# Reordering the opening, the early pairs' work and the d-weighted sums of a fused attention and two-MoE kernel

## The chip, the cores and the metric

The kernel runs on one core of a Trainium2 chip. The metric is device time in microseconds of one execution. Three executions of the kernel before took 804.86, 803.89 and 801.84 us (median 803.89). Half a percent of that is 4 us.

## The reference

Three blocks follow each other, all in float32.

```
k_p, v_p = mean of k, v over groups of 8 positions          # 8 batches, 8 heads, 576 -> 72 keys
attn     = softmax(q @ k_p.T / 8) @ v_p                     # 4608 tokens x 512 after merging heads
g        = relu(attn @ w_in) ** 2                           # 512 -> 2048
x        = g @ w_out                                        # 2048 -> 512
logits   = x @ phi                                          # 32 slots
d        = softmax of logits over the 4608 tokens
slots    = d.T @ x  ->  per expert relu(. @ w1) @ w2        # 8 experts, 4 slots each
out      = softmax(logits over the slots) @ slots
```

x itself is never needed by a token: logits are g @ (w_out @ phi) and d.T @ x is (d.T @ g) @ w_out. w_in and w_out arrive as float64 and are converted in the kernel.

## The kernel before, in words

The 4608 tokens are 36 tiles of 128 (t = 0 to 35). Attention for a tile runs in steps: att_qT (TensorE transposes of q, ScalarE copy), att_sc (scores on TensorE, maxima on VectorE, exps on ScalarE), att_norm (VectorE), att_aT and att_shift (turning the weights; on VectorE and ScalarE for t >= 12), att_av (TensorE; ScalarE makes the rounded half xh and VectorE the rest xl). The first MoE layer, h = x @ w_in, is split in four column quarters j. One tile and one quarter is a unit of 12 products (line 415, `l<-w,xh` and `l<-w,xl`): 144 units, 1728 products. Its PSUM bank has the tag l1, of which there are two. ScalarE's relu (L427) and a square, on VectorE for most units (L434), empty the bank, and SyncE stores g to DRAM (L438).

From tile 10 on, tiles go in pairs. For a pair and quarter, reload_turned brings g back in another layout, g_T turns it in blocks on VectorE (L475), and logits multiplies it by w_out @ phi on TensorE (L500). When the four quarters of a pair are in, log_T (L529) turns the logits, VectorE takes a running maximum (L532, L534), ScalarE the exps (L541), VectorE turns these into d (L544, L564), and dg (L574) adds d.T @ g on TensorE, which VectorE adds to acc (L584). log_T and dg share the one PSUM buffer `misc`. The pairs of tiles 0 to 9, here the early pairs, do this later, in between, from a copy of g read back from DRAM (`g_back`).

The order of the work is set in two stages. The loop over units runs half a unit at a time, and a table `ev` says at which of these slots (two to a unit, SLOTS = 8 to a tile) each other step is issued; post, post_end and attention fill it. The framework's scheduler then orders every engine's instructions by its own estimate, with the issue order as priority, and puts the semaphore waits in. `early` raises a priority; `behind`, `pinned` and `paced` hold a step back until a named instruction has been placed, and create no wait on the chip by themselves. Each engine runs its list in order.

The opening, before the steady loop, pools k and v of batch 0, runs attention for tiles 0 to 3 and converts the first two quarters of w_in. One conversion is one ScalarE step (L311), VectorE steps L313, L316, L320 and L325, one add (L324) that the letter in AE puts on VectorE (V) or GpSimd (P), a ScalarE cast (L363) and a GpSimd subtract (L364).

## Time and profile before

| | us |
|---|---|
| median of three executions | 803.89 |
| the profiled execution | 807.54 |
| its span, first to last instruction | 805.8 |
| TensorE busy | 754.0 (94%) |
| VectorE busy | 519.4 (64%) |
| ScalarE busy | 408.1 (51%) |
| GpSimd busy | 157.7 (20%) |

The profiled execution lies outside the span by 1.74 us and 3.65 us above the median. In the page's 40 slices of 20 us, TensorE is 60 to 70% busy in the first three and nearly full from there to the tail, which starts near 715 us. A TensorE that is called busy may still run at the lower of its two clock levels (1.2 and 2.4 GHz); the granted clock of a stretch shows that, 1.00 being the higher.

### The profile page before, as it was taken

Reading aid. Unit: us, or ns where it says so; the run is one execution under the profiler, and the core shown is the slowest. Engines: PE = TensorE matmul, PEld = TensorE weight load, DVE = VectorE, ACT = ScalarE, POOL = GpSimd, SP = SyncE. Lnnn points to the kernel's source line nnn. Section 1 sums busy time; section 2 is a strip of 40 time slices with the busy share of each in tenths; the row PEclk is TensorE's granted clock in tenths of the full one; section 3 lists DMA queues with packets and bytes.
Section 4 is the critical chain, followed back from the end, with each engine's and each line's share of the span. In section 5 each row is a group of like instructions: output and inputs, shape, how many; then the busy total and the mean of one; then the engine's idle time right before and its main releaser. Section 6 shows DMA issues by size and latency. Waiting matters only on the chain.

```text
span 805.8 us, 14370 instructions
## 1 busy us (share of the span) xinstructions
PE 754.0 (94%) x5352; PEld 521.4 (65%) x5352; DVE 519.4 (64%) x1016; ACT 408.1 (51%) x1161; POOL 157.7 (20%) x171
## 2 busy tenths in 40 slices
PE   6779999999999999999999999989999989998993
PEld 6557778767667766666667666656676756663552
DVE  5896855586827688697858677775688464324333
ACT  2755676443647364555546562654575533331232
POOL 1251412167514310071023403200000000000000
PEclk9799999999999999999999999989999999999996
DMA  8946753847835874985696696776457424969999
GB/s 258 287 144 193 233 145 124 264 125 226 260 118 159 250 220 119 297 251 145 205 293 203 180 301 187 201 220 193 118 181 249 120 79 176 349 242 321 371 372 312
DMA packets 177782, 175.07 MB, mean 217 GB/s; under 512 B 44080, under 2 KB 135216, under 8 KB 177712
## 3 DMA queue, kind: packets, MB, share of 16 engines
q1 hardware_dynamic: 177712, 174.16, 69.3%
q8 instruction: 42, 0.69, 0.4%
q14 instruction: 28, 0.23, 0.1%
HBM read 126.94 MB, written 47.19 MB: 216 GB/s over the span
## 4 chain that ended last, share of the span: by engine, by line
PE 71%; DVE 10%; DMA 8%; ACT 4%; POOL 3%; issue 2%; SPq 1%; POOLq 0%; ACTq 0%; DVEq 0%
PE l L415 42%; PE misc L574 4%; DMA kv<-in_v_dram 4%; PE pl L500 3%; PE misc L1006 2%; PE gT L280 2%; PE att L280 2%; PE gT L203 2%; PE l L974 2%; PE att L203 2%; PE att L500 2%; DMA st<-in_moe_w_in_dram 1%; DVE vp L160 1%; POOL kv L130 1%; DVE tmp L320 1%
## 5 line engine op out<-in xcount | busy, mean ns | idle before, releaser
L415 PE MATMUL l<-w,xh 128*128 128x512 f32 x1152 | 383.7, 412 | 8.5 <-DVE tmp L434 2.5
L415 PEld LDWEIGHTS l<-w,xh 128*128 128x128 f32 x1152 | 208.3, 190 | 83.1 <-issue 22.5
L415 PE MATMUL l<-w,xl 128*128 128x512 f32 x576 | 230.4, 400 | 0.0
L427 ACT ACTIVATE r<-l 128x512 f32<-128x512 f32 x144 | 86.4, 601 | 169.0 <-PE l L415 147.5
L415 PEld LDWEIGHTS l<-w,xl 128*128 128x128 f32 x576 | 108.9, 189 | 29.1 <-issue 3.7
L253 ACT COPY aT<-turned 32x256 f32<-32x256 f32 (+1 forms) x168 | 67.8, 404 | 16.7 <-DVE turned L262 14.1
L130 POOL TENSOR_TENSOR kv<-kv 72x512 f32<-72x512 f32 x40 | 53.7, 1346 | 72.1 <-DMA kv<-in_v_dram 53.2
L434 DVE TENSOR_TENSOR g<-l,r 128x512 f32<-128x512 f32 x57 | 38.8, 685 | 28.7 <-ACT r L427 20.4
L475 DVE STREAM_TRANSPOSE turned<-turned 128x1024 f32<-128x1024 f32 x39 | 47.7, 1230 | 2.9 <-DMA turned<-g_dram 2.9
L214 ACT ACTIVATE es<-gT,mx 128x72 f32<-128x72 f32 x120 | 36.9, 328 | 16.1 <-DVE mx L210 16.0
L214 ACT ACTIVATE es<-att,mx 128x72 f32<-128x72 f32 x120 | 37.0, 329 | 12.5 <-DVE mx L210 12.4
L255 DVE COPY aT<-turned 32x256 f32<-32x256 f32 (+1 forms) x120 | 40.2, 335 | 4.2 <-PE gT L280 2.3
L324 POOL TENSOR_TENSOR tmp<-tmp 128x512 f32<-128x512 f32 x20 | 28.0, 1399 | 68.5 <-DVE tmp L320 60.2
L132 POOL TENSOR_TENSOR kp<-kv 72x128 f32<-72x128 f32 x20 | 10.4, 538 | 142.8 <-PE att L173 142.7
L434 DVE TENSOR_TENSOR tmp<-l,r 128x512 f32<-128x512 f32 x33 | 22.7, 687 | 22.6 <-ACT r L427 16.6
L364 POOL TENSOR_TENSOR w<-tmp,w 128x512 fp32r<-128x512 f32 x16 | 24.8, 1562 | 55.9 <-ACT w L363 55.9
L436 ACT ACTIVATE g<-r 128x512 f32<-128x512 f32 x54 | 34.2, 636 | 0.9
L237 DVE TENSOR_TENSOR es<-es,rs 128x576 f32<-128x576 f32 x36 | 32.5, 903 | 0.8
L210 DVE TENSOR_REDUCE mx<-gT 128x4 f32<-128x288 f32 x38 | 16.5, 443 | 22.8 <-PE gT L203 22.6
L131 POOL TENSOR_TENSOR kv<-kv 72x256 f32<-72x256 f32 x40 | 30.7, 771 | 1.0
L475 DVE STREAM_TRANSPOSE tmp<-tmp 128x1024 f32<-128x1024 f32 x25 | 30.7, 1229 | 0.0
L203 PE MATMUL gT<-kb,qT 128*128 128x144 f32 (+1 forms) x176 | 26.4, 302 | 4.2 <-ACT qT L191 2.6
(188 smaller groups left out, 1139.7 us busy)
## 6 DMA issues: line engine op xcount, KB each, us to landing
g_dram<-g SPq DMA_DIRECT2D x95, 256.0 KB
turned<-g_dram SPq DMA_DIRECT2D x39, 512.0 KB
w<-in_moe_w_dram SPq DMA_DIRECT2D x32, 512.0 KB
tmp<-g_dram SPq DMA_DIRECT2D x25, 512.0 KB
w<-in_moe_w_dram SPq DMA_DIRECT2D x6, 2048.0 KB
kv<-in_k_dram SPq DMA_DIRECT2D x32, 288.0 KB
kv<-in_v_dram SPq DMA_DIRECT2D x32, 288.0 KB
out_dram<-o SPq DMA_DIRECT2D x36, 256.0 KB
```

Source lines behind the costliest of these rows:

```text
L130: eng.tensor_tensor(out=x[:, :, 0:4], in0=x[:, :, 0:4], in1=x[:, :, 4:8], op=ALU.add)
L203: mark["sc", t] = nc.tensor.matmul(sc[off:off + n, i * 2 * SP:(i + 1) * 2 * SP], qT[:, pi, off:off + n], kb[b % 2][:, pi].rearrange("p a s ...
L214: mark["es", t] = nc.scalar.activation(out=es[:, e], in_=sv[:, h], func=AF.Exp, bias=mx[:, e:e + 1], accum_out=rsum[:, t % 8, e, 0:1],)
L237: mark["norm", t] = nc.vector.tensor_tensor(out=es, in0=es, in1=rs.unsqueeze(2).to_broadcast([P, H, SP]), op=ALU.mult)
L253: nc.scalar.copy(out=dst, in_=src)
L255: eng[e].tensor_copy(dst, src)
L415: mark["l1", t, j] = nc.tensor.matmul(hp_t[t, j], steps[i][0], steps[i][1], start=(i == 0), stop=(i == 2 * n - 1))
L427: nc.scalar.activation(out=r, in_=hp, func=AF.Relu, scale=1.0 / (R * R if sq == "V" else R))
L434: mark["sq"] = nc.vector.tensor_tensor(out=dst, in0=pre, in1=src, op=ALU.mult)
L436: nc.scalar.activation(out=dst, in_=src, func=AF.Square)
L475: nc.vector.transpose(out=gc.rearrange("p (n i) -> p n i", i=32), in_=gc.rearrange("p (n f) -> p n f", f=32))
L500: mark["logits"] = nc.tensor.matmul(pl[32 * c:32 * c + 32], a_sb[:, c, 32 * j:32 * j + 32], gT[:, c], start=(alone or j == 0), stop=(alone ...
```

## The change

Seven edits, which move work and add only six warming products of the identity:

1. AE is all V: the four adds that were on GpSimd go to VectorE.
2. pool_v of batch 0 writes into a PSUM buffer of the tag l1 (two of them) and not into the one `misc`; att_qT of tile 1 is issued behind these products; six products on the identity are issued behind the transposes of tile 0's q.
3. In a slot, logits go first. Logits of an early pair are issued behind the latest logits, and the offsets of the early pairs move: g_T from 1 to 3, logits from 4 to 6, reloads from -4 to -2, dg from 22 to 23.
4. The later pairs' offsets move one slot ahead (logits 14 to 13, g_T 12 to 11, reloads 6 to 5, log_T 27 to 26, d_T 28 to 27).
5. dg of the pairs from tile 10 to before tile 28 is issued behind a first-layer product.
6. att_shift moves one slot ahead.
7. att_av, from unit slot 94 on, is issued behind the latest logits, for even tiles one slot ahead.

```diff
@@ -55,7 +55,7 @@
     EP = 3
     GO, LO = 3, 5
     PEP = (0, 1, 2)
-    AE = "VVVVVPVPPVVVVPVV"
+    AE = "V" * 16
     CS = ((2, 5, 7, 9), (13, 14, 15, 17))
 
     const = ctx.enter_context(tc.tile_pool(name="const", bufs=1))
@@ -148,9 +148,9 @@
         x = raw_v.pop((b, i))
         if b not in vp_t:
             vp_t[b] = pool.tile([SP, H, D], F32, tag="vp", name="vp", bufs=1)
-        pv = psm()[:SP, :2 * D]
+        pv = (ps("l1") if b == 0 else psm())[:SP, :2 * D]
         for r in range(R):
-            nc.tensor.matmul(pv, ident[:SP, :SP], x[:, :, r], start=(r == 0), stop=(r == R - 1))
+            mark["pv"] = nc.tensor.matmul(pv, ident[:SP, :SP], x[:, :, r], start=(r == 0), stop=(r == R - 1))
         nc.scalar.copy(out=vp_t[b][:, 2 * i:2 * i + 2].rearrange("p h d -> p (h d)"), in_=pv)
 
     def pool_v_dve(b, i, pool):
@@ -184,7 +184,7 @@
         qt = q_t.pop(t)
         pq = ps("gT" if t in (0, 2, 4, 6, 8, 10, 12, 14, 16, 18, 20, 22, 24, 26, 28, 29, 30, 31, 33) else "att")
         for i in range(NPAIR):
-            nc.tensor.transpose(
+            mark["q0"] = nc.tensor.transpose(
                 pq[:, i * P:(i + 1) * P], qt[:, 2 * i:2 * i + 2].rearrange("p h d -> p (h d)"), ident
             )
         qT = a1.tile([P, NPAIR, P], F32, tag="qT", name="qT")
@@ -343,6 +343,7 @@
 
     wq = []
     last_relu = []
+    last_l1 = []
 
     def paced(fn, *a):
         with tc.issue_after(last_relu[-1].ins):
@@ -412,7 +413,8 @@
         ]
         n = len(steps) // 2
         for i in range(half * n, (half + 1) * n):
-            mark["l1", t, j] = nc.tensor.matmul(hp_t[t, j], steps[i][0], steps[i][1], start=(i == 0), stop=(i == 2 * n - 1))
+            mm = mark["l1", t, j] = nc.tensor.matmul(hp_t[t, j], steps[i][0], steps[i][1], start=(i == 0), stop=(i == 2 * n - 1))
+        last_l1.append(mm)
         if half == 1:
             hp = hp_t.pop((t, j))
             if j == NQ - 1 and ND <= t < NT - 4:
@@ -712,19 +714,26 @@
             fn(*a)
 
     def run_slot(s):
-        for fn, a in ev.pop(s, []):
+        for fn, a in sorted(ev.pop(s, []), key=lambda e: e[0] is not logits):
             if fn in (g_T, logits, log_T, d_T, dg) and a[0] >= NT - EP:
                 early(fn, *a)
             else:
                 fn(*a)
 
+    def behind_l1(fn, *a):
+        with tc.issue_after(last_l1[-1].ins):
+            fn(*a)
+
     def pinned(name, fn, *a):
         with tc.issue_after(mark[name].ins):
             fn(*a)
 
     def post(t, s0, o, step=4):
         for j in range(NQ):
-            at(s0 + step * j + o[1], logits, t, j)
+            if t < ND:
+                at(s0 + step * j + o[1], pinned, "logits", logits, t, j)
+            else:
+                at(s0 + step * j + o[1], logits, t, j)
         for j in range(NQ):
             at(s0 + step * j + o[0], pinned, "sq", g_T, t, j)
             at(s0 + step * j + o[2], pinned, "store", reload_turned, t, j)
@@ -732,7 +741,10 @@
     def post_end(t, s0, p):
         at(s0 + p[0], log_T, t)
         at(s0 + p[1], d_T, t)
-        at(s0 + p[2], dg, t)
+        if ND <= t < NT - 8:
+            at(s0 + p[2], behind_l1, dg, t)
+        else:
+            at(s0 + p[2], dg, t)
 
     def attention(t, a0):
         if t >= NT - 4:
@@ -748,8 +760,11 @@
         at(a0 + 2, att_exp, t)
         at(a0 + 2, att_norm, t)
         at(a0 + 4, att_aT, t)
-        at(a0 + 6, att_shift, t)
-        at(a0 + 7, att_av, t)
+        at(a0 + 5, att_shift, t)
+        if a0 + 6 + t % 2 < 8 * ND + 14:
+            at(a0 + 7, att_av, t)
+        else:
+            at(a0 + 6 + t % 2, pinned, "logits", att_av, t)
 
     a_at = {4: 24, 5: 26}
     for t in range(6, NT):
@@ -779,8 +794,8 @@
         attention(t, a_at[t])
     for t in range(ND, NT - 2, 2):
         if t < NT - 4:
-            post(t, SLOTS * t, (12, 14, 6))
-        post_end(t, SLOTS * t, (27, 28, 28))
+            post(t, SLOTS * t, (11, 13, 5))
+        post_end(t, SLOTS * t, (26, 27, 28))
     for t in (NT - 4, NT - 2):
         s0 = SLOTS * t
         for i in range(2):
@@ -799,8 +814,8 @@
     for t in range(0, ND, 2):
         s0 = 96 + 28 * (t // 2)
         at(s0 - 5, reload_g, t)
-        post(t, s0, (1, 4, -4), 4)
-        post_end(t, s0, (20, 21, 22))
+        post(t, s0, (3, 6, -2), 4)
+        post_end(t, s0, (20, 21, 23))
     for b in range(1, B):
         s0 = a_at[b * S // P]
         for i in range(NPAIR):
@@ -871,6 +886,9 @@
         early(kb_from, 0, pk0)
         go(0, 0, 2)
         early(att_qT, 0)
+        warm = ps1.tile([P, P], F32, tag="pl", name="warm")
+        for _ in range(6):
+            behind(["q0"], nc.tensor.matmul, warm, ident, ident)
         go(0, 0, 1)
         behind([("qT", 0), "kbA"], go, 0, 0, 1)
         early(att_sc, 0)
@@ -890,7 +908,7 @@
         behind([("aT", 0)], go, 0, 3, 1)
         for half in range(2):
             l1_half(0, 0, half)
-        att_qT(1)
+        behind(["pv"], att_qT, 1)
         behind([("aT", 0)], att_sc, 1)
         att_norm(1)
         behind([("l1", 0, 0)], att_aT, 1)
```

TensorE, in the opening, from the scores of tile 0 to those of tile 1. `gT_262` and `att_381` are score buffers, `misc_291` and `misc_302` pooled v. Before:

```order
L203 MATMUL gT_262<-kb0_119,qT_255 128x144 x2
L203 MATMUL gT_270<-kb0_119,qT_255 128x144 x2
L153 MATMUL misc_291<-kv0_148,ident_93 72x128 x8
L187 MATMUL att_373<-ident_93,qt_155 128x128 x4
L153 MATMUL misc_302<-kv0_148,ident_93 72x128 x8
L203 MATMUL att_381<-kb0_119,qT_378 128x144 x2
L203 MATMUL att_389<-kb0_119,qT_378 128x144 x2
```

And in the changed kernel:

```order
L627 MATMUL warm_257<-ident_93 128x128 x6
L203 MATMUL gT_269<-kb0_119,qT_255 128x144 x2
L203 MATMUL gT_277<-kb0_119,qT_255 128x144 x2
L153 MATMUL l1_298<-kv0_148,ident_93 72x128 x8
L153 MATMUL l1_309<-kv0_148,ident_93 72x128 x8
L187 MATMUL att_380<-ident_93,qt_155 128x128 x4
L203 MATMUL att_388<-kb0_119,qT_385 128x144 x2
L203 MATMUL att_396<-kb0_119,qT_385 128x144 x2
```

Both poolings of v now stand ahead of the transposes of tile 1's q, and the six products stand ahead of the first scores.

TensorE, between units 103 and 104 of the first layer (near 526 us in the trace), where log_T and dg of the pair of tile 22 meet the attention of two tiles. Before:

```order
L203 MATMUL gT<-kb_119,qT 128x144 x4
L529 MATMUL misc<-plsb,s4rep 128x256
L187 MATMUL gT<-ident,qt 128x128 x4
L203 MATMUL gT<-kb_119,qT 128x144 x4
L574 MATMUL misc<-g,d 32x512 x2
L574 MATMUL misc<-tmp,d 32x512 x2
L574 MATMUL misc<-g,d 32x512 x3
L574 MATMUL misc<-tmp,d 32x512
```

And in the changed kernel, where the sums of an early pair (`g_back`), one unit earlier before, stand between the transposes of q and the scores:

```order
L203 MATMUL gT<-kb_119,qT 128x144 x4
L531 MATMUL misc<-plsb,s4rep 128x256
L187 MATMUL gT<-ident,qt 128x128 x4
L576 MATMUL misc<-g_back,d 32x512 x8
L203 MATMUL gT<-kb_119,qT 128x144 x4
L576 MATMUL misc<-g,d 32x512 x2
L576 MATMUL misc<-tmp,d 32x512 x2
L576 MATMUL misc<-g,d 32x512 x3
L576 MATMUL misc<-tmp,d 32x512
```

VectorE at the same place, from the scaling of one tile's exps (es0) to the square that gives unit 104 its PSUM bank (l1_5186 before, l1_5199 now). Before:

```order
L237 TENSOR_TENSOR es0_121<-es0_121,rs_5296 128x576
L210 TENSOR_REDUCE mx_5335<-gT_5336 128x4
L262 STREAM_TRANSPOSE turned_2429<-es0_121 128x768
L210 TENSOR_REDUCE mx_5335<-gT_5344 128x4
L434 TENSOR_TENSOR tmp_124<-l1_5186,r_5216 128x512
L255 COPY aT_5389<-turned_2429 32x8x32 x3
L255 COPY aT_5389<-turned_2429 8x8x32 x2
L584 SCALAR_TENSOR_TENSOR acc_101<-acc_101,scl_5179,misc_5198 128x512
```

And in the changed kernel:

```order
L237 TENSOR_TENSOR es0_121<-es0_121,rs_5306 128x576
L262 STREAM_TRANSPOSE turned_2436<-es0_121 128x768
L586 SCALAR_TENSOR_TENSOR acc_101<-acc_101,scl_5107,misc_5186 128x512
L255 COPY aT_5375<-turned_2436 32x8x32 x3
L255 COPY aT_5375<-turned_2436 8x8x32
L210 TENSOR_REDUCE mx_5343<-gT_5344 128x4
L255 COPY aT_5375<-turned_2436 8x8x32
L210 TENSOR_REDUCE mx_5343<-gT_5352 128x4
L436 TENSOR_TENSOR tmp_124<-l1_5199,r_5222 128x512
```

The five copies stood behind the square and now stand ahead of it, with an addition to acc (that of the early pair).

## Rows read from the trace of the kernel before

**Rows 1.** The page: the span, and busy time of each engine.
```profile
span 805.8 us, 14370 instructions
PE 754.0 (94%) x5352; PEld 521.4 (65%) x5352; DVE 519.4 (64%) x1016; ACT 408.1 (51%) x1161; POOL 157.7 (20%) x171
```

**Rows 2.** Windows: length, busy us (instructions) by engine, granted clock, DMA.
```profile
0.00:63.00 63.00, 44.63 (x403) 36.34 (x403) 46.64 (x87) 33.59 (x96) 19.62 (x27) 0.92 0.72 220
...
230.00:715.00 485.00, 477.09 (x3022) 321.42 (x3021) 326.60 (x681) 255.35 (x747) 72.85 (x90) 0.99 0.65 200
...
20.40:56.60 36.20, 26.92 (x162) 20.49 (x162) 32.92 (x57) 23.80 (x78) 13.29 (x10) 0.86 0.68 214
```

**Rows 3.** Timeline of TensorE, opening: start, us, instruction, idle before and releaser.
```profile
21.74 1.11 PE L187 MATMUL att<-ident,qt 128*128 128x128 f32 x4 [3.99 <-DMA qt<-in_q_dram]
24.91 3.69 PE L153 MATMUL misc<-kv,ident 72*72 72x128 f32 x16 [2.05 <-ACT vp L154]
...
62.95 1.19 PE L415 MATMUL l<-w,xh 128*128 128x512 f32 x4 [0.89 <-ACT xh L287]
```

**Rows 4.** Windows of 2 us in the opening, for the granted clock.
```profile
24.00:26.00 2.00, 1.09 (x5) 1.10 (x6) 1.76 (x3) 1.35 (x5) 1.21 (x1) 0.50 0.99 288
```

**Rows 5.** Timeline of VectorE, opening.
```profile
12.43 0.69 DVE L324 TENSOR_TENSOR tmp<-tmp 128x512 f32<-128x512 f32 x1
...
15.65 1.64 DVE L324 TENSOR_TENSOR tmp<-tmp 128x512 f32<-128x512 f32 x1
...
35.88 1.74 DVE L325 SCALAR_TENSOR_TENSOR tmp<-tmp 128x512 uint32<-128x512 uint32 x1
...
55.17 1.40 DVE L237 TENSOR_TENSOR es<-es,rs 128x576 f32<-128x576 f32 x1
```

**Rows 6.** Timeline of GpSimd at the same times.
```profile
35.79 1.28 POOL L364 TENSOR_TENSOR w<-tmp,w 128x512 fp32r<-128x512 f32 x1 [1.47 <-ACT w L363]
...
54.29 1.66 POOL L324 TENSOR_TENSOR tmp<-tmp 128x512 f32<-128x512 f32 x1 [2.09 <-DVE tmp L320]
```

**Rows 7.** Timeline of TensorE near 110 us, before unit 16.
```profile
112.55 1.14 PE L280 MATMUL att<-aT,vp 72*64 72x128 f32 x16 [0.59 <-ACT aT L269]
```

**Rows 8.** Timeline around 562 us: a chain from log_T to d without a queue.
```profile
561.71 0.63 PE L415 MATMUL l<-w,xh 128*128 128x512 f32 x2
562.17 0.60 PE L529 MATMUL misc<-plsb,s4rep 128*128 128x256 f32 x2
...
565.44 0.74 DVE L564 STREAM_TRANSPOSE d<-dT 32x64 f32<-32x64 f32 x3
```

**Rows 9.** Timeline between units 103 and 104, the pair of tile 22.
```profile
519.65 1.92 PE L574 MATMUL misc<-g_back,d 128*32 128x512 f32 x16
...
527.72 0.66 PE L187 MATMUL gT<-ident,qt 128*128 128x128 f32 x4 [0.98 <-ACT es L214]
...
530.05 2.29 PE L203 MATMUL gT<-kb,qT 128*128 128x144 f32 x8 [1.68 <-ACT qT L191]
...
534.27 0.69 DVE L434 TENSOR_TENSOR tmp<-l,r 128x512 f32<-128x512 f32 x1 [0.28 <-PE misc L574]
...
534.88 1.46 DVE L255 COPY aT<-turned 32x256 f32<-32x256 f32 x5
...
535.84 0.97 PE L415 MATMUL l<-w,xh 128*128 128x512 f32 x2
...
536.37 0.75 DVE L584 SCALAR_TENSOR_TENSOR acc<-acc,scl,misc 128x512 f32<-128x512 f32 x1
```

**Rows 10.** A window of 4 us at the same place, for the granted clock.
```profile
532.00:536.00 4.00, 4.00 (x19) 0.76 (x17) 3.65 (x9) 3.14 (x13) 0.00 (x0) 0.50 0.04 9
```

**Rows 11.** Timeline around unit 128, the pair of tile 28.
```profile
642.46 0.59 PE L529 MATMUL misc<-plsb,s4rep 128*128 128x256 f32 x2
...
648.56 0.62 PE L574 MATMUL misc<-g,d 128*32 128x512 f32 x2 [1.22 <-DVE d L564]
...
651.71 0.74 PE L415 MATMUL l<-w,xh 128*128 128x512 f32 x2 [1.22 <-DVE tmp L434]
```

## The prediction

> **What bounds the kernel now.** The page comes first: TensorE is busy 754.0 of 805.8 us and no other engine comes near [rows 1]. The windows by stage come second, since that share is an average. In the steady stretch from 230 to 715 us TensorE is busy 477.09 of 485 us; in the first 63 us it is busy 44.63, and there VectorE is busy longer, 46.64 [rows 2]. So two regimes matter. In the opening VectorE's list sets the pace: from 20.4 to 56.6 us it is busy 32.92 of 36.2 us [rows 2]. In the steady part every us of TensorE's idle time, and every stretch at the lower clock level, lands in the end; all other work there is hidden. Third is TensorE's timeline, for idle times with their releasers. In the opening the reader is to see 3.99 us before the transposes of tile 1's q and 2.05 us before the second pooling of v, and then that pooling taking 3.69 us [rows 3], at a granted clock of 0.50, the lower level [rows 4]. In the steady part two places stand out: between units 103 and 104 idle times of 0.98 and 1.68 us [rows 9], and at unit 128 two of 1.22 us [rows 11]. The change touches all of these. The end of the kernel, from the last pairs on, keeps its order and counts as nothing.
>
> **Opening, edits 1 and 2.** Seen from TensorE alone much goes: the second pooling moves into the wait for q, and the scores of tile 1, which stood behind it, no longer wait. But the first dense unit group starts at 62.95 us behind xh of tile 3 [rows 3], and this comes at the end of VectorE's list. So I sum that list over 20.4 to 56.6 us, to the last of the four scalings (L237). By the changed order the same piece holds three more adds (L324, 0.69 us each [rows 5]) and two more last steps L325, which stood just behind the piece before; I price these at 0.65: 3.4 us more. Against that, VectorE is drawn out while GpSimd works: an L325 takes 1.74 us beside a GpSimd subtract of 1.28 us, and a scaling 1.40 us beside a GpSimd add of 1.66 us [rows 5, 6]. Against some 0.7 us undisturbed, as the add at 12.43 us [rows 5], that is 1.0 and 0.7 us. Three GpSimd adds leave the piece, 2.1 to 3.0 us less. Last, VectorE's idle time there was 36.2 - 32.92 = 3.3 us; in the changed list I find some 0.7 us, for the exps of tile 0 end earlier. The piece becomes 3.4 - (2.1 to 3.0) - 2.6 = -1.3 to -2.2 us by this sum. Some of it is lost behind it: ScalarE's list now has two turned tiles, two squares and two casts ahead of xh of tile 3. I take -0.8. The bounds: -4.0, if the wait of 3.99 us for q turns wholly into gain, and +3.0, since the changed list puts xl of tile 0 behind nine more VectorE operations, of 0.36 to 0.69 us and one lengthened, while ScalarE gives xh no earlier. The six warming products stand where TensorE waits for the copies of the pooled k, so at no cost; they have a quarter of the columns of a first-layer product, which takes 0.23 us (two in 0.46 [rows 8]), and without that cover I estimate 1.5 us at most.
>
> The rows show the delay beside GpSimd as 0.7 to 1.0 us an operation [rows 5, 6]. The Trainium skill ("SBUF — State Buffer", "Who interferes with whom") says that a VectorE instruction with two SBUF inputs and a GpSimd instruction that reads SBUF exclude each other for the whole instruction. By that rule the moved adds have the same exposure to the subtracts that stay, and the trace agrees: the add at 15.65 us took 1.64 us [rows 5]. By the rule alone a GpSimd operation could cost VectorE its full 1.28 to 1.66 us, three of them 3.8 to 5.0, and the piece would be shorter by 3.0 to 4.2 us; by the rows it is the -1.3 to -2.2 above.
>
> **Unit 16.** The average over v of one tile waits 0.59 us for its turned weights [rows 7]. In the changed order these weights are turned later: only nine of sixteen products of another average (0.65 us of 1.15) and four transposes (0.66) stand between. The wait grows by up to 0.9 us; I take +0.6, bounds 0 and +0.9.
>
> **The pair of tile 12 (unit 64), edits 3 to 5.** log_T of this pair slips behind an early pair's sums, since both need `misc`, and dg follows after 3.4 us of TensorE work: one average (1.14 us [rows 7]), four short transposes, log_T itself and seven products at 0.23 us. Before, there were over 7 us between. A chain from log_T to d without a queue takes from 562.17 to 566.18, 4.0 us [rows 8]; where exps stand in its way, 642.46 to 648.56, 6.1 us [rows 11]. The wait is 0.6 us at least and 2.7 at most. VectorE's list holds only the chain itself there, so I take +0.6.
>
> **The pair of tile 22 (units 103 and 104).** Before, dg followed log_T by two steps of attention alone, and unit 104 began at 535.84 us [rows 9]. The sums of the early pair (1.92 us at 519.65 [rows 9]) now fill the wait for the scaled q, which was 1.68 us. But unit 104 needs the PSUM bank that the square at 534.27 empties, and by the changed list five copies (1.46 us) and an addition to acc (0.75 us) come ahead of that square [rows 9]. Without its 0.28 us of idle time the square would end at 534.27 + 0.69 - 0.28 + 1.46 + 0.75 = 536.9 us, 1.05 us after unit 104's old start; with 1.92 us of work already in, the net is -0.9. TensorE would then stand idle for some 3 us in front of unit 104, where before it worked, at the lower level (0.50 [rows 10]). Before, that level fell on a stretch which waited anyway; now it may fall on dense products. A window of 4 us at 0.50 costs 2 us, two of them 4. Bounds -0.9 and +3.0; I take +0.7, nearer to the row of 0.50, with most of one such window.
>
> **The pair of tile 28 (unit 128).** log_T stood 12 products and little else ahead of dg, 3.7 us of TensorE work; now 22 products, two score steps and four logits, 6.3 us, more than the 6.1 us that the chain took [rows 11]. The first 1.22 us go. The second was a square queued behind d, the turn of a tile and its copies; in the changed list the square stands ahead of these. Both go: -2.4, and -1.2 if the square is late.
>
> **The rest.** Edit 4 keeps six slots between a reload and its turn, so the DMAs have the time they had. The turns of an early and a later pair now fall into one slot and stand side by side on VectorE; the square behind them has a second PSUM bank as cover. Price nothing, at most 1.5 us over the whole part.
>
> **Sum.** -0.8 + 0.6 + 0.6 + 0.7 - 2.4 = -1.3 us. The profiled execution took 807.54 us with a span of 805.8; it becomes 806.2. It stood 3.65 us above the median of three, and I set the change against that median: 803.89 - 1.3 = 802.6 us.
>
> **Rivals.** What a measurement can tell from no change is 0.5%, 4 us: below 799.9 or above 807.9 us.
>
> First, the opening really shrinks. TensorE's chain for tile 1 and half of the time at the lower level go, and xh of tile 3 comes near 59 us. For it: 6 us of waits in [rows 3] are removed by name. Against it: VectorE's busy 91% of the piece. Price -4.0 in place of -0.8, and the pair of tile 22 at -0.9: 803.9 - 6.1 = 797.8 us.
>
> Second, slower, at one place: VectorE's list in front of unit 104. If the attention of the second tile keeps the square until after 537 us and the idle TensorE falls to the lower level for two windows, the term is +3.0, and the same pattern of copies ahead of squares, which the changed list shows at two more places (pairs of tiles 12 and 14, 9 us of VectorE work between two squares, by my count of the list, for 7 before), costs 1.5 each. Then 803.9 - 1.3 + 2.3 + 3.0 = 807.9, and above it if the low stretch is longer. It decides from 6 us of idle time and slow products at the three places together, since the other terms sum to -2.0. Against it: before, runs of 8 to 10 us of VectorE work between squares showed no wait at other places.
>
> Third, the adds are not paid back. If GpSimd's subtracts, now four in a row, draw out the moved adds as the one at 15.65 us, and tile 0's xl is late, the opening is +3.0: 806.4 us, with one of the waits above at its upper end 808.
>
> **How the numbers follow.** Forecast, all near their middle: 0.44. First rival 0.32. Second 0.17, third 0.07. So faster 0.32, same 0.44, slower 0.24. The range runs from just under the first rival, 797.0, to just above the second, 808.5; beyond them I leave 0.2. The likeliest case alone has 800 to 806.
>
> **What would show it.** Right: the first dense group starts between 60 and 64 us; at unit 128 no wait above 0.4 us for d or for a square; a wait for a square of 2 to 4 us in front of unit 104. Wrong: the dense group starts before 60 us; no wait in front of unit 104 at all; or new waits of TensorE for d or a square above 1.5 us between 340 and 500 us. The prediction fails if any one place moves more than 4 us.

## The result, and the profile after

The kernel after took 796.42 us (median of four executions, 794.55 to 799.82) beside 804.38 for the kernel before: a ratio of 0.9912, 95% interval 0.989 to 0.9934. Timed again later (e9 below), it took 796.76 us, ratio 0.9882 (0.9859 to 0.9905). By the medians it is faster by 8.0 us, and by 9.4 in e9. The forecast, 802.6, was too high, and the time is 0.6 us below the foot of the range. Of all executions below one, of e6, took 1800.86 us and is left out of that kernel's ratio.

First the page's busy times of the profiled execution, which took 799.82 us:

```profile
PE 753.3 (94%) x5364; PEld 528.1 (66%) x5364; DVE 515.6 (65%) x1020; ACT 407.1 (51%) x1161; POOL 149.8 (19%) x167
```

TensorE is busy as long as before [rows 1] in a span that is 7.8 us shorter. The windows that answer to [rows 2] (length, busy us of TensorE, its loads, VectorE, ScalarE and GpSimd, then granted clock):

```profile
0.00:63.00 63.00, 51.07 (x418) 42.74 (x419) 46.44 (x94) 34.11 (x98) 16.51 (x25) 0.84 0.76 229
230.00:707.00 477.00, 470.11 (x3018) 321.28 (x3017) 325.86 (x681) 254.89 (x747) 73.60 (x90) 1.00 0.67 203
20.40:56.60 36.20, 28.45 (x169) 21.94 (x168) 36.13 (x66) 24.15 (x80) 10.09 (x8) 0.86 0.72 230
```

In the first 63 us TensorE stands idle for 11.9 us, where it was 18.4, but at a mean clock of 0.84 for 0.92: part of the filled time is work at the lower level. Its busy time there is 6.4 us longer than before [rows 2], so that behind the first 63 us it is some 7 us shorter. VectorE is now busy without a gap in the piece of the opening that the prediction summed, 36.13 of 36.2 us. TensorE's timeline of the opening, for [rows 3]:

```profile
26.28 1.25 PE L203 MATMUL att<-kb,qT 128*128 128x144 f32 x8 [1.51 <-ACT qT L191]
...
29.86 1.47 PE L268 MATMUL gT<-ident,es 128*72 128x128 f32 x8 [2.33 <-DVE es L237]
...
62.19 1.20 PE L416 MATMUL l<-w,xh 128*128 128x512 f32 x4
```

The wait of 3.99 us for the q of tile 1 is gone, and the pooling of 3.69 us no longer stands behind it; 1.51 and 2.33 us stand near by instead, the second for VectorE. The first dense group starts at 62.19 us for 62.95. The places of [rows 7] and of the pair of tile 12 (unit 64):

```profile
111.05 1.14 PE L280 MATMUL att<-aT,vp 72*64 72x128 f32 x16
...
341.66 0.62 PE L576 MATMUL misc<-g,d 128*32 128x512 f32 x2 [0.69 <-ACT r L429]
```

The wait of 0.59 us at unit 16 is gone, and one of 0.69 us stands in front of dg at unit 64. Between units 103 and 104, for [rows 9]:

```profile
524.59 0.66 PE L187 MATMUL gT<-ident,qt 128*128 128x128 f32 x4 [0.98 <-ACT es L214]
...
527.41 2.39 PE L576 MATMUL misc<-g_back,d 128*32 128x512 f32 x16 [2.16 <-DVE lt_sb L546]
...
531.95 0.69 PE L576 MATMUL misc<-g,d 128*32 128x512 f32 x2
...
534.12 0.73 PE L416 MATMUL l<-w,xh 128*128 128x512 f32 x2 [0.18 <-DVE tmp L436]
```

Here the 1.68 us for the scaled q has become 2.16 us in front of the early pair's sums (`g_back`), which cannot start until VectorE has turned the logits of the later pair out of `misc`. In front of unit 104 only 0.18 us are left (0.94 in the trace of e9), for this square:

```profile
533.38 0.69 DVE L436 TENSOR_TENSOR tmp<-l,r 128x512 f32<-128x512 f32 x1
```

Two windows of 4 us there, for [rows 10]:

```profile
527.00:531.00 4.00, 3.59 (x21) 1.77 (x22) 3.82 (x10) 0.77 (x2) 0.00 (x0) 0.72 0.26 58
531.00:535.00 4.00, 3.82 (x25) 1.87 (x24) 3.83 (x10) 3.93 (x19) 0.00 (x0) 0.86 0.91 291
```

The granted clock there is 0.72 and 0.86, where [rows 10] had 0.50. Around unit 128, for [rows 11]:

```profile
633.47 0.70 PE L531 MATMUL misc<-plsb,s4rep 128*128 128x256 f32 x2
...
641.22 0.62 PE L576 MATMUL misc<-g,d 128*32 128x512 f32 x2
```

dg follows log_T by 7.75 us of other work and waits for nothing; the next first-layer products do not wait either.

Counted by the starts of units (12 first-layer products each, in TensorE's timeline), the two profiled executions differ like this: unit 4 starts 2.1 us earlier, unit 44 0.4, unit 100 1.8, unit 135 7.5, and the rest of the kernel keeps that. So in this pair of traces nearly all is gained between units 44 and 135, and 5.8 us of it behind the start of unit 104 (1.7 us earlier).

### The profile page after: what moved, and what is told of

It reads as the page before. It is cut to its first block, busy times and chain, and to the rows that moved or that the text cites. A ratio compares the mean times of both kernels' runs of the same rounds, so it can differ in the third digit from the quotient of the medians.

```text
span 798.0 us, 14389 instructions
## 1 busy us (share of the span) xinstructions
PE 753.3 (94%) x5364; PEld 528.1 (66%) x5364; DVE 515.6 (65%) x1020; ACT 407.1 (51%) x1161; POOL 149.8 (19%) x167
## 4 chain that ended last, share of the span: by engine, by line
PE 75%; DVE 9%; DMA 6%; ACT 3%; issue 3%; POOL 2%; SPq 1%; ACTq 0%; DVEq 0%; POOLq 0%
PE l L416 44%; PE pl L502 3%; PE misc L576 3%; PE gT L280 2%; PE misc L1024 2%; DMA kv<-in_v_dram 2%; PE att L280 2%; PE l L992 2%; PE gT L203 2%; DMA kv<-in_k_dram 2%; PE att L203 2%; PE att L137 2%; PE att L502 2%; DMA qt<-in_q_dram 1%; PE misc L531 1%
## 5 line engine op out<-in xcount | busy, mean ns | idle before, releaser
L255 DVE COPY aT<-turned 32x256 f32<-32x256 f32 (+1 forms) x120 | 37.5, 312 | 4.0 <-PE gT L280 2.3
L365 POOL TENSOR_TENSOR w<-tmp,w 128x512 fp32r<-128x512 f32 x16 | 22.9, 1433 | 70.2 <-ACT w L364 70.2
L313 DVE TENSOR_SCALAR tmp<-tmp 128x512 uint32<-128x512 uint32 x32 | 22.4, 701 | 16.8 <-ACT tmp L311 16.7
L324 POOL TENSOR_TENSOR tmp<-tmp 128x512 f32<-128x512 f32 x16 | 21.1, 1321 | 62.2 <-DVE tmp L320 62.2
L237 DVE TENSOR_TENSOR es<-es,rs 128x576 f32<-128x576 f32 x36 | 30.1, 837 | 0.9
L311 ACT ACTIVATE tmp<-st 128x512 f32<-128x512 f32 x32 | 21.4, 672 | 13.6 <-DMA st<-in_moe_w_in_dram 9.5
```

Source lines behind the costliest of these rows:

```text
L255: eng[e].tensor_copy(dst, src)
```

## The experiments

Twelve kernels ran, in three groups of four, each with the kernel before beside it. All numbers of a stretch below go from the start of unit 44 to the start of unit 135 (the first-layer products 529 and 1621 in TensorE's order) of the kernel's own profiled execution, so each holds the same work. "Breaks" counts, in TensorE's list of instructions, how often the run of first-layer products is left for other products in that stretch.

### The opening against the rest: e1 and e2

e1 is the kernel before with edits 1 and 2 (its diff cut to the lines that do the work):

```diff
-    AE = "VVVVVPVPPVVVVPVV"
+    AE = "V" * 16
-        pv = psm()[:SP, :2 * D]
+        pv = (ps("l1") if b == 0 else psm())[:SP, :2 * D]
...
+        for _ in range(6):
+            behind(["q0"], nc.tensor.matmul, warm, ident, ident)
...
-        att_qT(1)
+        behind(["pv"], att_qT, 1)
```

> The kernel before with edits 1 and 2 alone (the adds on VectorE, the opening's buffers, order and six warm products); the later units as before. The first theory (the opening gives about 2 us at unit 4, and the rest of the gain of 8 us comes from the stretch behind 230 us): unit 4 starts 2 us earlier, at most 2 us of it is left at the end, so about 802.5 us beside 804.4, a ratio of 0.997 to 1.000. The rival that the opening gives nearly all: about 797 us, ratio 0.991.

Measured: 801.18 us, ratio 0.9962 (0.9939 to 0.9985). e2 is the rest, edits 3 to 7 of the diff, on the opening of before (cut in the same way):

```diff
+        for fn, a in sorted(ev.pop(s, []), key=lambda e: e[0] is not logits):
...
+                at(s0 + step * j + o[1], pinned, "logits", logits, t, j)
...
+            at(s0 + p[2], behind_l1, dg, t)
...
+        at(a0 + 5, att_shift, t)
...
+            at(a0 + 6 + t % 2, pinned, "logits", att_av, t)
...
+            post(t, SLOTS * t, (11, 13, 5))
...
+        post(t, s0, (3, 6, -2), 4)
```

> The kernel before with edits 3 to 7 alone (order of logits, av, turn and sums with d); the opening as before. The first theory: unit 44 to unit 135 take 6.5 to 7.5 us less, as in the kernel after, so about 797.5 us, ratio 0.990 to 0.993. The rival that the opening gives nearly all: about 803.5 us, ratio 0.998 to 1.000.

Measured: 797.08 us, ratio 0.9914 (0.9887 to 0.9941), as good as the whole change. TensorE's list in the stretch is the same in e2 and in the kernel after, so the first theory holds: the first rival of the prediction (the opening) does not carry the result. By itself the opening does give something, and more than the first theory allowed (a ratio of 0.9962, where it had 0.997 at the least). But e1's executions fall in two halves: six at a mean granted clock of 0.977 to 0.982 took 798.4 to 800.2 us, six at 0.970 to 0.976 took 802.1 to 805.7, and the profiled one is of the second half.

In e1 the stretch also took only 420.7 us, with the order of before, whose own profile has 423.8. So a single trace of before is some 2 us high in this stretch, and what the edits do must be read against several traces with the old order: 420.7 in e1, 421.3 and 422.8 in e3 and e4 below, mean 421.6.

### The two parts of the opening: e3 and e7

```diff
# e3: edit 1 alone
-    AE = "VVVVVPVPPVVVVPVV"
+    AE = "V" * 16
# e7: edit 2 alone, the other lines of e1
```

> The kernel before with edit 1 alone: the seven adds of the opening that GpSimd made are on VectorE. First theory: VectorE is the busier engine of the opening with them, but what the first units wait for is no longer behind GpSimd, so unit 4 starts 1 to 2 us earlier and the time falls by 0 to 2 us, ratio 0.9975 to 1.000; edit 2 then adds at most 1 us to it. Rival: the adds alone are not hidden on VectorE, the time rises by 1 to 4 us, ratio 1.001 to 1.005, and edit 2 with its warm products and order is what pays.

> The kernel before with edit 2 alone (the pooling of v in the l1 buffers, q of tile 1 behind it, six warm products). First theory (VectorE's list sets the opening): unit 4 starts within 1 us of the kernel before, since the three GpSimd adds and what they draw out stay; about 804 us, ratio 0.9985 to 1.001. Rival (TensorE's chain for tile 1 sets it): unit 4 starts 2 to 4 us earlier, 801 us, ratio 0.995 to 0.9975.

(The letters of AE move four adds, not seven.) Measured: e3 803.31 us, ratio 0.9985 (0.9964 to 1.0005); e7 805.43, ratio 1.001 (0.9989 to 1.0031). By time neither alone can be told from no change. In the traces unit 4 starts at 62.7 us in e3 and at 67.0 in e7; with the opening of before it starts between 65.7 and 68.2 us (five traces). Edit 2 alone gives nothing that can be measured, as the first theory had it. But e7 is not the old order behind the opening: the scheduler gave TensorE another list in the stretch, although the edit stands in the opening. In its trace both waits at unit 128 are gone, without an edit there, and a wait for a square of the kind that the prediction feared stands in front of unit 104:

```profile
534.37 1.22 PE L415 MATMUL l<-w,xh 128*128 128x512 f32 x2 [2.85 <-DVE tmp L434]
...
638.83 0.60 PE L529 MATMUL misc<-plsb,s4rep 128*128 128x256 f32 x2
...
647.21 0.62 PE L574 MATMUL misc<-g,d 128*32 128x512 f32 x2
```

The stretch takes 421.5 us all the same. So the two waits of unit 128 can go and the kernel be no faster.

With both edits, unit 4 starts anywhere between 61.8 and 67.2 us, and e1 shows why. The end of VectorE's list there, the start of the dense group, and three windows:

```profile
51.87 0.76 DVE L237 TENSOR_TENSOR es<-es,rs 128x576 f32<-128x576 f32 x1
```

```profile
62.27 2.08 PE L415 MATMUL l<-w,xh 128*128 128x512 f32 x4
```

```profile
0.00:20.00 20.00, 15.57 (x206) 14.63 (x206) 10.14 (x28) 5.99 (x15) 3.94 (x16) 1.00 0.91 266
56.00:64.00 8.00, 7.78 (x66) 6.52 (x63) 3.02 (x6) 3.50 (x8) 1.26 (x1) 0.53 0.49 135
64.00:68.00 4.00, 4.00 (x13) 3.12 (x13) 1.93 (x1) 0.18 (x1) 0.00 (x0) 0.67 0.09 7
```

VectorE's last scaling ends at 52.6 us, 4 us earlier than before (55.17 + 1.40, [rows 5]): the shortening that the first rival wanted. But from 56 to 68 us TensorE runs at 0.53 and 0.67, four products take 2.08 us and not 1.19 [rows 3], and unit 4 starts at 67.2 us as if nothing had been gained. In e3 the window from 56 us is at the full clock:

```profile
58.70 1.20 PE L415 MATMUL l<-w,xh 128*128 128x512 f32 x4 [1.05 <-ACT xh L287]
```

```profile
56.00:64.00 8.00, 6.95 (x85) 5.68 (x82) 6.82 (x9) 4.05 (x10) 2.83 (x2) 1.00 0.71 209
```

Here the dense group starts at 58.7 us, near the 59 of the first rival. Of the six traces with both edits three have the low stretch behind 56 us (e1, e10, e11, to within 0.1 us of each other). In the two of the kernel after it falls early, in the first 20 us,

```profile
0.00:20.00 20.00, 16.45 (x170) 15.88 (x171) 5.78 (x22) 5.02 (x8) 3.96 (x16) 0.75 0.89 257
56.00:64.00 8.00, 7.25 (x88) 5.84 (x89) 5.11 (x8) 5.54 (x12) 2.71 (x2) 1.00 0.50 131
```

and there VectorE's last scaling ends at 56 to 57 us. In one, e8, neither happens, and unit 4 starts at 61.8 us. What decides where the lower level falls was not tried.

### Edit 5 alone: e4

```diff
+        if ND <= t < NT - 8:
+            at(s0 + p[2], behind_l1, dg, t)
...
```

> The kernel before with edit 5 alone: the product for dg of tiles 10 to 27 is issued behind a first-layer product. First theory (the gain of the later stretch is spread: fewer changes between first-layer and other products, a higher clock at unit 104, one wait): this edit alone changes less than 2 us, ratio 0.9975 to 1.001. Rival (the gain is the removed waits at units 104 and 128 alone, which edit 5 takes away by itself): unit 104 starts 3 us or more earlier relative to unit 100, and the time falls by 3 to 6 us, ratio 0.9925 to 0.996.

Measured: 803.96 us, ratio 0.9994 (0.9977 to 1.0011). The two waits of 1.22 us at unit 128 are still there in its trace, the same to the hundredth. The rival falls.

### Edits 3 and 4, and edits 6 and 7: e5, e6 and e11

```diff
# e5: edits 3 and 4
-            post(t, SLOTS * t, (12, 14, 6))
-        post_end(t, SLOTS * t, (27, 28, 28))
+            post(t, SLOTS * t, (11, 13, 5))
+        post_end(t, SLOTS * t, (26, 27, 28))
-        post(t, s0, (1, 4, -4), 4)
+        post(t, s0, (3, 6, -2), 4)
# e6: edits 6 and 7; e11: these with edits 1 and 2
-        at(a0 + 6, att_shift, t)
-        at(a0 + 7, att_av, t)
+        at(a0 + 5, att_shift, t)
+        if a0 + 6 + t % 2 < 8 * ND + 14:
+            at(a0 + 7, att_av, t)
+        else:
+            at(a0 + 6 + t % 2, pinned, "logits", att_av, t)
```

> The kernel before with edits 3 and 4 alone (logits first in a slot, early pairs' logits behind the latest logits, offsets moved; later pairs one slot ahead). First theory (the waits): the two waits of 1.22 us at unit 128 go with the earlier log_T and the earlier square, and nearly all of the gain of the middle edits sits there, so units 100 to 135 take 170 to 171 us beside 173.3 to 175.3 in the kernels with the old order, and the time is 799 to 801 us, ratio 0.993 to 0.996. Rival (the grouping of the attention steps): these edits take 2.4 us off unit 128 and give it back elsewhere, 803 us, ratio 0.998 or more.

> The kernel before with edits 6 and 7 alone (att_shift one slot ahead; att_av behind the latest logits, even tiles one slot ahead). First theory (the waits): the two waits of 1.22 us at unit 128 stay; fewer changes between first-layer and other products give 0.5 to 1.5 us, about 803.5 us, ratio 0.998 to 1.000. Rival (the grouping of the attention steps is what pays): L187, L203 and L280 take 1.7 us less between units 100 and 135, first-layer products 1 us less, and with the same elsewhere the time is 799 to 801 us, ratio 0.993 to 0.996.

> The kernel before with edits 1, 2, 6 and 7: the kernel after without edits 3 to 5. First theory (the attention's edits carry the stretch from unit 44 to 135, 417.4 us alone for 417.0 with edits 3 to 5, and edits 3 to 5 add nothing to them): the same time as the kernel after within 1.5 us, ratio 0.988 to 0.9925. Rival (the effects add: 0.9952 for edits 3 and 4 and 0.9923 for 6 and 7): 3 us or more slower than the kernel after, ratio 0.992 to 0.995.

Measured: e5 801.41 us, ratio 0.9952 (0.9932 to 0.9973); e6 798.71, ratio 0.9923 (0.9896 to 0.995); e11 797.33, ratio 0.9887 (0.9861 to 0.9913), beside 0.9882 for the kernel after on the same chip. So the attention's two edits give most by themselves, both parts remove the same waits, and edits 3 to 5 add nothing measurable to edits 6 and 7. The first theory of e6 (the waits stay, ratio 0.998 or more) fell. In e6, where log_T and dg kept their slots, the waits at unit 128 are gone too:

```profile
633.42 0.70 PE L529 MATMUL misc<-plsb,s4rep 128*128 128x256 f32 x2
...
641.18 0.62 PE L574 MATMUL misc<-g,d 128*32 128x512 f32 x2
...
643.04 0.50 PE L415 MATMUL l<-w,xh 128*128 128x512 f32 x1
```

log_T stands 7.8 us ahead of dg, where [rows 11] had 6.1. And the long wait at unit 104 comes with edits 3 and 4 (edit 3 moves the early pair's sums); in e5 it is the same 2.16 us, with the sums behind it slower (3.64 us for 2.39 in all, the first half of them shown here) at a clock of 0.50:

```profile
528.47 1.93 PE L574 MATMUL misc<-g_back,d 128*32 128x512 f32 x8 [2.16 <-DVE lt_sb L544]
```

```profile
528.00:532.00 4.00, 3.53 (x16) 0.68 (x16) 3.79 (x12) 0.71 (x2) 0.00 (x0) 0.50 0.27 60
```

This is where edits 3 to 5 lose what they gain. Units 100 to 105 take 28.4 us in e6 and e11, at a granted clock of 1.00, and 32.0 and 32.7 in the kernel after and e9, where one stretch at the lower level falls there (0.6 us of the difference is a logits group that falls on this side of unit 100). The rest of the stretch takes 387.4 and 388.9 us in e6 and e11, and 384.6 and 384.2 in the kernel after and e9.

### What a break costs: e8, e9 and e10

e8 is the kernel after with the four logits products of a later quarter cut in two:

```diff
+        if split(t):
+            logits_mm(t, j, 0, 2)
+        else:
+            logits_mm(t, j, 0, 4)
+            logits_out(t, j)
+    def logits_rest(t, j):
+        with tc.issue_after(last_l1[-1].ins):
+            logits_mm(t, j, 2, 4)
+        logits_out(t, j)
+                at(s0 + step * j + o[1] + 1, logits_rest, t, j)
```

> The kernel after, with the four logits products of each quarter of the pairs from tile 10 to before tile 32 cut in two halves, the second one slot later behind a first-layer product: no product added, 44 more breaks in the run of first-layer products. First theory (each change from first-layer products to others and back costs about 0.1 us and 0.1 us of TensorE, which is how the kernel after saves time without a wait): 44 x 0.21 = 9 us more than the kernel after, 804 to 806 us, ratio to before 1.000 to 1.003; first-layer and logits products in the trace take that much longer. Rival (a change costs nothing beyond the products' own time, the shorter times are an accident of which records show): 796 to 798 us, ratio 0.990 to 0.993.

Measured: 812.38 us, ratio 1.0103 (1.007 to 1.0136), slower than either theory. It does not tell them apart: most halves landed beside other work, so that the list has only nine breaks more, and the time went elsewhere. The busy time of the logits in the stretch, in e8 and in the kernel after:

```profile
251.57:684.13 432.56, 57.02 (x536) 15.64 (x536) 1.00 0.65 195
```

```profile
257.26:673.93 416.67, 43.98 (x536) 12.34 (x536) 1.00 0.68 203
```

and one quarter whole in the kernel after, with the first-layer products around it, two halves in e8:

```profile
325.81 0.63 PE L416 MATMUL l<-w,xh 128*128 128x512 f32 x2
326.27 0.40 PE L416 MATMUL l<-w,xl 128*128 128x512 f32 x1
326.60 0.64 PE L502 MATMUL pl<-turned,a_sb 128*32 128x256 f32 x8
327.17 0.73 PE L416 MATMUL l<-w,xh 128*128 128x512 f32 x2
327.73 0.40 PE L416 MATMUL l<-w,xl 128*128 128x512 f32 x1
```

```profile
323.16 0.63 PE L514 MATMUL pl<-turned,a_sb 128*32 128x256 f32 x4
...
325.31 0.62 PE L514 MATMUL pl<-turned,a_sb 128*32 128x256 f32 x4
```

Half of the products takes as long as all: 0.63 us for four records, 0.64 for eight (a product leaves two records). The four products of a quarter, each to 32 output partitions of its own, run beside each other; cut apart, they lose that, 57.02 - 43.98 = 13.0 us of busy time in the stretch. The Trainium skill ("TensorE: Matmul & The Clock Gate", "Part 3: Packing small matmuls — row/col tiling") says that products on different 32-column tiles of the array overlap; these rows agree.

e10 goes the other way, two quarters at a time; e9 is the kernel after beside it.

```diff
-                at(s0 + step * j + o[1], logits, t, j)
+                at(s0 + step * (j | 1) + o[1], logits, t, j)
```

> The kernel after with the logits of the pairs from tile 10 to before tile 32 two quarters at a time (the first of two waits four slots for the second): the same products, and in the order of TensorE 147 breaks in the run of first-layer products in place of 163. First theory (each break costs 0.2 to 0.3 us of TensorE, as the 14 fewer between units 44 and 135 of the kernel after went with 4.2 us less of busy time): 3 to 5 us less than the kernel after, units 44 to 135 in 413.5 to 415.5 us, with first-layer products 2 us or more below 273.3. Rival (breaks cost nothing by themselves; only waits and the attention's own steps count): the same as the kernel after within 1 us, or slower where a turned tile is held longer and its reload waits.

> The kernel after once more, timed on the same chip as the three kernels beside it: ratio to before 0.989 to 0.993, units 44 to 135 in 417 to 419 us.

Measured: e10 794.44 us, ratio 0.9868 (0.9845 to 0.9892); e9 796.76, ratio 0.9882. The stretch: all of TensorE, then its first-layer products alone, in e1 (order of before), after, e9 and e10.

```profile
256.11:676.83 420.72, 415.23 (x2648) 278.84 (x2646) 297.53 (x630) 226.28 (x670) 61.70 (x78) 1.00 0.66 201
```

```profile
256.11:676.83 420.72, 285.71 (x1093) 197.39 (x1093) 1.00 0.66 201
```

```profile
257.26:673.93 416.67, 410.84 (x2648) 280.25 (x2646) 299.24 (x630) 226.17 (x670) 63.42 (x78) 1.00 0.68 203
```

```profile
257.26:673.93 416.67, 282.10 (x1093) 198.43 (x1093) 1.00 0.68 203
```

```profile
256.21:673.06 416.85, 410.42 (x2647) 279.51 (x2646) 298.76 (x630) 226.30 (x670) 63.08 (x78) 1.00 0.67 202
```

```profile
256.61:672.50 415.89, 412.32 (x2647) 281.26 (x2646) 298.91 (x630) 226.67 (x670) 63.34 (x78) 1.00 0.68 203
```

```profile
256.61:672.50 415.89, 277.90 (x1092) 199.53 (x1093) 1.00 0.68 203
```

The first-layer products, the same 1092 in each (a row can count one more at its edge), were busy 285.71, 282.10 and 277.90 us with 116, 102 and 86 breaks. All kernels but e8, by the same two rows each:

| kernel | breaks | stretch, us | TensorE idle | first-layer busy |
|---|---|---|---|---|
| before | 116 | 423.8 | 6.8 | 285.9 |
| e1, e3, e4 (old order) | 116 | 420.7, 421.3, 422.8 | 5.5, 5.8, 7.2 | 285.7, 285.7, 285.7 |
| e7 (edit 2) | 116 | 421.5 | 6.2 | 287.2 |
| e6, e11 (edits 6, 7) | 113 | 415.7, 417.2 | 3.2, 4.6 | 284.7, 284.7 |
| e5 (edits 3, 4) | 107 | 419.1 | 4.6 | 283.4 |
| e2, after, e9 | 102 | 415.6, 416.7, 416.9 | 5.3, 5.8, 6.4 | 282.1, 282.1, 282.1 |
| e12 (without edit 2) | 98 | 414.9 | 4.9 | 281.0 |
| e10 | 86 | 415.9 | 3.6 | 277.9 |

From 116 to 86 breaks the first-layer time falls from 285.7 to 277.9 us, 0.26 us a break, and no kernel leaves the line by more than 0.3 us but e7, where the lower level fell on first-layer products of unit 104. Since the end of a busy row overlaps the start of the next, I also summed from start to start without the idle times: 274.3 us at 116 (e1, e3, e4), 271.8 at 102, 269.7 at 86, which is 0.15 us a break. The rows around one quarter above show it: within the run two products take 0.46 us from start to start (325.81 to 326.27), but the one before the logits leaves 0.33 us for 0.23 and the first two behind them take 0.56 (327.17 to 327.73).

That a break costs the first-layer products 0.15 us or more is shown. That the kernel gains as much for each break that goes is not. With 16 breaks fewer than e9, all of TensorE in e10 was busy 1.9 us longer (412.32 for 410.42), its logits alone 47.85 us for 43.98, because they were taken apart in more places. Its stretch is 1.0 us shorter than that of e9 only by idle time, and the lower level did not fall there at all. The theory's 3 to 5 us did not come, and by time e10 cannot be told from the kernel after. And e6, with 113 breaks, needs no longer for the stretch than the kernel after with 102.

### Without edit 2: e12

```diff
# the kernel after, with these put back
+        pv = psm()[:SP, :2 * D]
+        att_qT(1)
# and without mark["q0"], mark["pv"] and the six warm products
```

> The kernel after without edit 2 (edits 1 and 3 to 7). First theory (edit 2 gives nothing, as alone, 1.001; the adds on VectorE give the little that the opening gives): the same time as the kernel after within 1.5 us, unit 4 at 63 to 65 us, ratio 0.988 to 0.9925. Rival (edit 2 pays once the adds are moved, 0.9962 for both beside 0.9985 for the adds alone): 2 us slower, ratio 0.992 to 0.995.

Measured: 794.96 us, ratio 0.9869 (0.9846 to 0.9893), the same as the kernel after within the intervals. Unit 4 starts at 63.6 us. Edit 2 pays nothing that can be measured; as in e7, the order of the stretch changed with it (98 breaks for 102).

## Why the prediction was right and wrong

The likeliest case had the direction right and the size wrong: it gave -1.3 us, which it counted as no change, and the kernel is faster by 8.0 us (9.4 in e9), about 1%. The first rival's 797.8 us lies near the measured 796.42 by luck: it put 4 us on the opening, and e2 is as fast without the opening's edits.

**The step that failed is "The rest. Price nothing."** The prediction went through the waits of TensorE and called all its other time fixed. Read against three traces with the old order (e1, e3, e4), the stretch went from 421.6 to 416.8 us (after and e9); the idle time in it did not change, 6.2 us before and 6.1 after. The whole 4.8 us is busy time: first-layer products 285.7 to 282.1, logits 45.0 to 44.0, averages over v (L280) 29.1 to 28.05, these being busy sums that overlap a little. The first part goes with the fewer breaks, 14 at 0.17 (start to start) to 0.26 us, 2.4 to 3.6 us. That the shorter logits and averages have the same cause was not tried by itself. Nor is this the only way to the same time: in e6 and e11 the gain is in good part idle time (3.2 and 4.6 us) and the clock at unit 104, with three breaks fewer than before. The diff said it plainly: logits first in a slot, early logits behind later ones, averages behind logits put three kinds of work side by side, and I read that only for whom it makes wait.

**The opening, -0.8.** Right in the profiled execution, but by luck: the dense group is 0.76 us earlier there, and 0.4 us later in e9 (63.34 us), the same kernel. The working was not right. The sum for VectorE's list, -1.3 to -2.2, was too small: where TensorE's first 20 us run at the full clock, the list ends 4 us earlier (e1), and the lower level takes that back later. The prediction had the lower level as a cost only at unit 104. Of the drawing out I said 0.7 to 1.0 us for each GpSimd operation. The kernel after shows it on other instructions, first VectorE's, then GpSimd's:

```profile
25.85 1.42 DVE L316 TENSOR_SCALAR tmp<-tmp 128x512 uint32<-128x512 uint32 x1
...
52.30 1.30 DVE L324 TENSOR_TENSOR tmp<-tmp 128x512 f32<-128x512 f32 x1
```

```profile
25.65 1.34 POOL L365 TENSOR_TENSOR w<-tmp,w 128x512 fp32r<-128x512 f32 x1 [6.04 <-ACT w L364]
...
51.59 1.46 POOL L365 TENSOR_TENSOR w<-tmp,w 128x512 fp32r<-128x512 f32 x1 [2.22 <-ACT w L364]
```

Of the nine subtracts between 18 and 58 us seven have such an instruction beside them, 0.4 to 1.0 us longer than its like; one of them is a moved add. Each of the seven ends a fixed time behind the subtract that was running when it began: 0.28 us for L313 and L316 (27.27 behind 26.99 in the rows above), 0.55 us for L320, L324 and L325 (53.60 behind 53.05). So it waits for the rest of the subtract, and there is no price for each GpSimd operation; its loss depends on how much of the 1.26 to 1.65 us is left when it comes. The Trainium skill ("SBUF — State Buffer", "Who interferes with whom") says that whichever of the two engines comes first holds the ports that they share for its whole instruction, while the other waits; these rows agree. The prediction took from that rule a full operation each, which is its upper bound.

**Unit 16, +0.6:** wrong, no wait is left there (111.05 us). **Unit 64, +0.6:** the size is right, 0.69 us; the profile puts it down to a relu on ScalarE and not to d, so the reason is not confirmed.

**The pair of tile 22, +0.7:** the wait of 2 to 4 us came, but at another place and for another reason. I forecast it in front of unit 104 for a square. It stands in front of the early pair's sums, 2.16 us, because log_T and the sums share the one `misc` buffer, a fact that the prediction used at unit 64 and forgot here. The square itself ended at 533.38 + 0.69 = 534.1 us and cost 0.18. Beside the old order the place is worth nothing: units 100 to 105 take 32.0 us (32.7 in e9), and 31.9 to 32.0 in e1, e3 and e4 (33.3 in the trace of before, where the low level at [rows 10] fell longer). Beside e6 and e11, with 28.4, it costs some 3 us. The second rival's slower case did not come as a whole.

**The pair of tile 28, -2.4:** right in size and place; both waits went. But e6 shows that the averages' new place does it as well as the earlier log_T, which the prediction gave as the cause, and in e7 they went without either.

**New waits, within "at most 1.5 us":** the removed 2.4 us at unit 128 were matched by others, 0.69 us at 341.66, 2.16 for 1.68 at unit 104, smaller ones, and one for pooled v from GpSimd, so that the idle time is the same:

```profile
367.39 1.09 PE L280 MATMUL gT<-aT,vp 72*64 72x128 f32 x16 [1.04 <-POOL kv L130]
```

**What stays open.** The traces account for at most 2 us in the opening and 4.8 in the stretch, 5 to 7 us; the times say 8.0 (5.3 to 8.8) and 9.4 (7.6 to 11.4). The first interval takes this in, the second does not quite. Traces of one order differ by 2 to 3 us, so the rest could not be placed. What part of the 4.8 us the breaks are worth to the kernel stays open too.

## What to carry to other kernels

When TensorE is busy nearly all the time, a list of its waits is not the whole price of a reordering: count also how often the change makes it leave its main run of products and how it takes apart products that run side by side, price both from the start-to-start times in the trace, and hold TensorE's whole busy time beside it, since one kind of product can gain what another loses. Let a stretch begin and end at the same product in every trace, and read it in several traces with the same order before a difference of 3 us in it is put down to an edit. Compare the engines' whole lists too: an edit in one place can change the scheduler's order in another. And look for one buffer that two steps share whenever one of them is moved next to the other.

## What the runs showed of the hardware that was not expected

- The same 1092 first-layer products were busy 285.7 us with 116 breaks and 277.9 with 86: 0.26 us a break, 0.15 from start to start. TensorE as a whole did not gain that in e10.
- Four products to 32 output partitions each take 0.64 us together, and two of the four still 0.63 us; cutting the later pairs' quarters so cost 13 us of busy time in the stretch.
- A VectorE instruction that met a running GpSimd subtract ended 0.28 us (L313, L316) or 0.55 us (L320, L324, L325) behind the subtract's end, whenever it had begun; all fourteen traces show these two figures to within 0.01 us.
- The same opening, in kernels that differ only behind it, meets the lower clock level at different times: unit 4 started at 61.8 us where 56 to 68 us ran at 1.00 (e8), and at 67.2 us where it ran at 0.53 and 0.67 (e1, e10, e11).
- Executions of the kernel after follow the mean granted clock: 0.971 to 0.973 with 797.9 to 799.8 us, 0.980 to 0.981 with 793.8 to 795.0 us.
